# Linear attention and two MLPs on one core: ScalarE issues the stores of prepared weights, TensorE's order is written out in the direct blocks, and the last direct block's sums leave PSUM to other slots

## The chip, the cores and the metric

The kernel runs on one core of one Trainium2 chip. The metric is device time in microseconds (us), taken as the median of three runs. A core has five engines with an instruction queue each: TensorE (PE; PEld is its weight load), VectorE (DVE), ScalarE (ACT), GpSimd (POOL) and SyncE (SP), which computes nothing and issues DMAs. An engine works its queue in the order in which it was written; where an instruction waits for a semaphore, what is queued behind it waits too.

## What is computed

```python
q_s = softmax(q, over head_dim);  k_s = softmax(k, over seq)     # 8 batches, 8 heads, 576 x 64
kv  = einsum('bhsd,bhse->bhde', k_s, v)
x   = einsum('bhsd,bhde->bhse', q_s, kv)  -> 4608 tokens x 512
x   = relu(x @ w_in)**2 @ w_out                                  # 512 -> 2048 -> 512
out = (silu(x @ w_gate) * (x @ w_val)) @ w_out2                  # 512 -> 1536 -> 512
```

All arrays are float32 but the weights come in as 64-bit floats, whose bits are turned into float32 on the chip. Each float32 operand is split into a high half (`L116`, a cast on ScalarE) and a low half (`L117`, a subtraction on VectorE or GpSimd), and each product is three matmuls, high x high, high x low, low x high (`L122`, `mm3`).

## The kernel before

The 4608 tokens are nine blocks of 512. Blocks 0 to 4 go through the first MLP directly; blocks 5 to 8 in two pairs, each with seven products in place of eight (a Strassen scheme of halves); then the second MLP runs over five groups of blocks in the same scheme.

**Block 0** (to about 130 us) has an order written out by hand on all engines. **Blocks 1 to 4** (`for n in range(NF, NE * NF + LAG)`) have one step for each of the 16 slices f of the hidden layer: `h_mm` makes 12 matmuls into PSUM tile ph, `g_of` turns them into g (Relu, Square and the cast on ScalarE, the low half on VectorE), and `acc_mm` of the slice before (LAG = 1) adds 12 matmuls into four accumulators. Between them stands a tick of a clock (`first_tick`), two in each step, 128 in the four blocks. A tick runs what is due: a part of `kv_unit` and `q_unit` (attention of batches and blocks to come: loads of k, v and q, exponentials, transposes, sums; its result x goes to DRAM array x1d one tick late, through `store` and `flush`), the loads of the next block's x (`x_loads`, three ticks ahead of its first step), and a step or two of `work`.

**`work`** prepares weight operands. For the first MLP, 16 items (`first_operands`): load two tiles wsum from DRAM, four sums and differences on GpSimd, then two stages. For the second, 18 items (`operands`): load wraw, convert the bits (wbits), sums, then four stages. A stage takes the staging tile wst (one buffer in these blocks), splits a source into it and stores it to DRAM in one or two stores of 256 KB (arrays hd, ad, gvd, od). Two stages of a `first_operands` item hold two stores each; of an `operands` item, three hold two and one holds one. `Stream.fetch` loads these operands (wu) later, ahead of the products of the pairs and groups.

Order: SyncE issues in the order of the program everywhere (`manual_schedule(engines={SP})` around all). In block 0 every engine does, in the pairs TensorE does too. In blocks 1 to 4 a planner sets the order of TensorE, VectorE, ScalarE and GpSimd by its own model of their times.

Stores of operands go through `store` (L238 to L241), on SyncE at once while `hold[0]` is 0, which is so until the end of block 4. In the pairs `hold[0]` is 2: a store is put into `late` and issued two ticks later by `flush` (L243 to L246). After an `operands` item, `if late` makes two empty steps and a flush.

Slots: pool cv has one tag, wbits, with five buffers, for wbits, wsum, e of `q_unit`, the tiles of `x_loads` (four a block), x of the first pair (`x_begin`: four for c = 0, then four for c = 1) and e of `x2_store`, where each block's four accumulators leave PSUM. rp (tag r) and gp (tag g) have two buffers each and are used by `g_of`. After block 4 the accumulators' PSUM banks go to the pairs.

Of the kernel before, what the change touches and what calls it, by code (L numbers as in the profile page):

```python
# [8 lines left out]
F32 = mybir.dt.float32  # L9
F32R = mybir.dt.float32r  # L10
# [7 lines left out]
P = 128  # L18
# [4 lines left out]
def tile_linear_attention_two_mlps(  # L23
# [29 lines left out]
    nc = tc.nc  # L53
# [4 lines left out]
    T = 512  # L58
    TJ = T // P
    NB = NT // T  # L60
    NP = H // 2
    NF = FF // P
# [6 lines left out]
    def f32(ap):  # L69
        return ap.bitcast(F32)  # L70
# [166 lines left out]
    def store(to, src, ticks=0):  # L237
        if ticks:  # L238
            late.append((clock.now + ticks, to, src))
        else:  # L240
            nc.sync.dma_start(to, src)  # L241

    def flush(until=None):  # L243
        for x in list(late):
            if until is None or x[0] <= until:
                nc.sync.dma_start(x[1], x[2])  # L246
                late.remove(x)

    stages = [(stp, "wst")]
    staged = [0]  # L250
    hold = [0]

    def stage():
        pool, tag = stages[staged[0] % len(stages)]
        staged[0] += 1
        if len(stages) == 1:
            flush()
        return pool.tile([P, 2, 2, U], F32R, name="wst", tag=tag)

    made = set()  # L260
# [1 line left out]
    def operands(kind, f):  # L262

        w, by_rows = {"gate": (w_gate, False), "val": (w_val, False), "out": (w_out2, True)}[kind]
        raw = []
        for s in (f, NG + f):
            t = raws.tile([P, T], w.dtype, name="wraw", tag="wraw")
            raw_load(w, by_rows, s, t)
            raw.append(t)
        yield  # L270
        first, = bits_of(raw[:1])
        yield
        second, = bits_of(raw[1:])
        yield
        a, b = first[:, 0:U], first[:, U:2 * U]
        c, d = second[:, 0:U], second[:, U:2 * U]

        def sums(n):
            t = cv.tile([P, T], F32, name="wsum", tag="wbits")
            return t, t[:, 0:U], t[:, U:2 * U]  # L280

        def tt(to, x, y, op):
            nc.gpsimd.tensor_tensor(to, x, y, op=op)  # L283

        if by_rows:

            m, t1, t3 = sums(0)
            n, t2, t4 = sums(1)
            tt(t1, b, a, ALU.subtract)
            tt(t3, d, b, ALU.subtract)  # L290
            tt(t2, t3, a, ALU.add)
            tt(t4, c, t2, ALU.subtract)
            todo = ((first[:, 0:U], ("1",)), (second, ("2", "3")), (m, ("5", "7")), (n, ("6", "4")))
        else:

            m, s1, s3 = sums(0)
            n, s2, s4 = sums(1)
            tt(s1, c, d, ALU.add)
            tt(s3, a, c, ALU.subtract)
            tt(s2, d, s3, ALU.subtract)  # L300
            tt(s4, b, s2, ALU.subtract)
            todo = ((first, ("1", "2")), (second[:, U:2 * U], ("4",)), (m, ("5", "7")), (n, ("6", "3")))
        yield
        for source, names in todo:
            k_ = len(names)
            t = stage()
            src = source.rearrange("p (k n) -> p k n", k=k_)
            hi, lo = t[:, 0:k_, 0], t[:, 0:k_, 1]
            if by_rows:
                src = src.rearrange("p k (x e) -> p k x e", e=2)  # L310
                hi, lo = (y.rearrange("p k (e x) -> p k x e", e=2) for y in (hi, lo))
            split(hi, lo, src, nc.gpsimd if k_ == 1 else None)
            for j, name in enumerate(names):
                if by_rows:
                    to = od[PRODUCTS.index(name)][:, f]
                else:
                    to = gvd[f][:, 2 * PRODUCTS.index(name) + (kind == "val")]
                store(to, f32(t[:, j]), hold[0])
            yield
        if late:  # L320
            yield
            yield
            flush()
        made.add((kind, f))

    def all_operands():
# [6 lines left out]
    def first_to(kind, f, name):  # L333
        n = PRODUCTS.index(name)
        return hd[f // 2][:, 2 * n + f % 2] if kind == "in" else ad[n][:, f]

    def first_operands(kind, f):

        m, n = (cv.tile([P, T], F32, name="wsum", tag="wbits") for _ in range(2))
        for x, t in enumerate((m, n)):  # L340
            nc.sync.dma_start(t, w1d[kind][f][:, x])
        yield
        a, b, c, d = m[:, 0:U], m[:, U:2 * U], n[:, 0:U], n[:, U:2 * U]

        def tt(to, x, y, op):
            nc.gpsimd.tensor_tensor(to, x, y, op=op)  # L346

        if kind == "in":
            tt(a, a, c, ALU.subtract)
            tt(c, c, d, ALU.add)  # L350
            tt(d, d, a, ALU.subtract)
            tt(b, b, d, ALU.subtract)
            todo = (m, ("7", "3")), (n, ("5", "6"))
        else:
            tt(d, d, b, ALU.subtract)
            tt(b, b, a, ALU.subtract)
            tt(a, d, a, ALU.add)
            tt(c, c, a, ALU.subtract)
            todo = (m, ("6", "5")), (n, ("4", "7"))
        yield  # L360
        for source, names in todo:
            t = stage()
            split(t[:, :, 0], t[:, :, 1], source.rearrange("p (k n) -> p k n", k=2))
            for j, name in enumerate(names):
                store(first_to(kind, f, name), f32(t[:, j]))
            yield
        made.add((kind + "1", f))

# [152 lines left out]
    def q_transpose(i, hp):  # L521
        pt = ps_a.tile([P, T], F32, name="pa", tag="pa")
        src = qs.pop((i, hp)).rearrange("p j h d -> p j (h d)")
        for j in range(TJ):
            nc.tensor.transpose(pt.rearrange("r (p j) -> r j p", j=TJ)[:, j], src[:, j], ident)
        t = qtp.tile([P, 2, T], F32R, name="qT", tag=f"qT{hp % 2 if i == 1 else 0}")
        split(t[:, 0], t[:, 1], pt)
        qT[i, hp] = t

    def x_sums(px, i, hp):  # L530
        t = qT.pop((i, hp))
        for p0, n, b, _ in runs(i):
            kv = kvs[b % 2]
            c = slice(p0 * TJ, (p0 + n) * TJ)
            mm3(px[:, c], (kv[:, hp, 0], kv[:, hp, 1]), (t[:, 0, c], t[:, 1, c]), True, True)

    def x_slice(i, hp, src):
        x = xp.tile([P, 2, T], F32R, name="xT", tag="xT")
        split(x[:, 0], x[:, 1], src)
        xT[i, hp] = x  # L540
# [57 lines left out]
            clock.at(s - 1, lambda hp=hp: load_q(i, hp))  # L598
            clock.at(s + 1, lambda hp=hp: q_unit(i, hp))

    gT, acc = {}, {}

    def h_mm(i, f):
        ph = ps_h.tile([P, T], F32, name="ph", tag="ph")
        for c in range(NP):
            x = xT[i, c]
            mm3(ph, w1.pair(("in", f), c), (x[:, 0], x[:, 1]), c == 0, c == NP - 1)
        return ph
# [9 lines left out]
    def acc_mm(i, f, d):  # L618
        if f == 0:
            acc[i, d] = ps_acc.tile([P, T], F32, name="acc", tag="acc")  # L620
        g = gT[i, f]
        mm3(acc[i, d], w1.pair(("out", f), d), (g[:, 0], g[:, 1]), f == 0, f == NF - 1)

    def x2_store(i, d):
        e = cv.tile([P, T], F32, name="e", tag="wbits")
        if d % 2:
            nc.vector.tensor_copy(e, acc.pop((i, d)))
        else:
            nc.scalar.copy(e, acc.pop((i, d)))  # L629
        nc.sync.dma_start(x2d[i][:, d], e)  # L630
# [371 lines left out]
    with tc.manual_schedule(engines={mybir.EngineType.SP}):  # L1002
# [236 lines left out]
            for steps in x_steps:  # L1239
                next(steps, None)  # L1240

        for n in range(NF, NE * NF + LAG):
            i, f = divmod(n, NF)
            a = divmod(n - LAG, NF)
            if i < NE:
                if f == 0:
                    for hp in range(NP):
                        if i == 1:
                            px = ps_h.tile([P, T], F32, name="ph", tag="ph")
                            x_sums(px, i, hp)  # L1250
                            x_slice(i, hp, px)
                            if hp + 2 < NP:
                                q_transpose(i, hp + 2)
                        else:
                            x_slice(i, hp, qT.pop((i, hp)))
                        acc_mm(*a, hp)
                ph = h_mm(i, f)
                first_tick()
                g_of(i, f, ph)
            if not (f == 0 and i < NE):  # L1260
                for d in range(NP):
                    acc_mm(*a, d)
            if a[1] == NF - 1:
                for d in range(NP):
                    x2_store(a[0], d)
            if i < NE:
                first_tick()
                if clock.now > LAST - 8:
                    stream.fetch()
        for _ in x_steps[0]:  # L1270
            pass
        ph1.close()
# [3 lines left out]
        pools["ps6"] = st_first.enter_context(  # L1276
            tc.tile_pool(name="ps6", bufs=1, space=PSUM, reuse_waits="tile")
        )
        hold[0] = 2
        for p in range(len(pairs)):  # L1280
            if p:
                stages.extend(((qtp, "qT0"), (qtp, "qT1")))
# [94 lines left out]
```

## Time and profile before

| | us |
|---|---|
| median of 3 runs | 1856.49 (1851.72 to 1860.39) |
| the profiled execution, its own time | 1851.19 |
| span of that execution, first to last instruction | 1849.1 |
| TensorE busy | 1680.8 (91%) |
| VectorE busy | 1112.2 (60%) |
| ScalarE busy | 871.9 (47%) |
| GpSimd busy | 462.5 (25%) |

Busy time is an average over stages with different limits. The profile says more by stage: block 0 to 130 us, blocks 1 to 4 to 702 us, the pairs and the first gated products to about 1164 us, and the rest. Where an engine is idle, the trace names what ended its wait. SPq stands for SyncE's queue. An idle engine costs nothing unless it is the one that the end waits for.

### The profile page before, as it was taken

Reading aid. Unit: us, or ns where it says so; the run is one execution under the profiler, and the core shown is the slowest. Engines: PE = TensorE matmul, PEld = TensorE weight load, DVE = VectorE, ACT = ScalarE, POOL = GpSimd, SP = SyncE. Lnnn points to the kernel's source line nnn. Section 1 sums busy time; section 2 is a strip of 40 time slices with the busy share of each in tenths; the row PEclk is TensorE's granted clock in tenths of the full one; section 3 lists DMA queues with packets and bytes.
Section 4 is the critical chain, followed back from the end, with each engine's and each line's share of the span. In section 5 each row is a group of like instructions: output and inputs, shape, how many; then the busy total and the mean of one; then the engine's idle time right before and its main releaser. Section 6 shows DMA issues by size and latency. Waiting matters only on the chain.

```text
span 1849.1 us, 23986 instructions
## 1 busy us (share of the span) xinstructions
PE 1680.8 (91%) x8210; PEld 1364.8 (74%) x8210; DVE 1112.2 (60%) x1775; ACT 871.9 (47%) x1520; POOL 462.5 (25%) x428
## 2 busy tenths in 40 slices
PE   7999937975996988998999899999999999999999
PEld 5787725654765766786777678788888888888898
DVE  8964324435455545858676866864476368446746
ACT  7764414434444444545455554543363346334434
POOL 4752222222121232225222233301200110021010
PEclk9999958986998998999999999999999999999999
DMA  9946665455546457787788889886678677766797
GB/s 303 282 159 228 211 210 162 141 156 168 162 123 187 137 187 212 219 262 269 246 286 310 292 285 307 308 247 209 214 217 240 194 216 217 237 195 204 226 380 273
DMA packets 275017, 419.99 MB, mean 227 GB/s; under 512 B 126288, under 2 KB 167248, under 8 KB 274896
## 3 DMA queue, kind: packets, MB, share of 16 engines
q1 hardware_dynamic: 274352, 418.33, 71.0%
q8 instruction: 66, 1.08, 0.2%
q14 instruction: 55, 0.45, 0.1%
q10 hardware_dynamic: 544, 0.13, 0.0%
HBM read 317.19 MB, written 101.19 MB: 226 GB/s over the span
## 4 chain that ended last, share of the span: by engine, by line
PE 59%; DMA 10%; DVE 8%; POOL 5%; ACT 4%; issue 4%; SPq 4%; POOLq 0%; DVEq 0%; ACTq 0%
PE ps L122 51%; PE ph L122 4%; PE acc L122 3%; POOL wsum L346 2%; DMA wsum<-w1d_out 2%; DVE wst L117 1%; SPq L467 1%; ACT wst L116 1%; DMA qs<-in_q_dram 1%; SPq L241 1%; DVE uo L117 1%; POOL qs L547 1%; DMA wraw<-in_moe_w_val_dram 1%; DMA wraw<-in_moe_w_out_dram 1%; DMA wraw<-in_moe_w_gate_dram 1%
## 5 line engine op out<-in xcount | busy, mean ns | idle before, releaser
L122 PE MATMUL ps<-w,wu 128*128 128x512 f32 (+1 forms) x3192 | 680.6, 375 | 16.7 <-ACT e L629 11.6
L122 PEld LDWEIGHTS ps<-w,wu 128*128 128x128 f32 x3192 | 566.8, 189 | 126.4 <-ACT e L629 12.3
L122 PE MATMUL ps<-uo,wu 128*128 128x512 f32 (+1 forms) x1932 | 428.1, 382 | 18.1 <-DVE uo L117 18.0
L122 PEld LDWEIGHTS ps<-uo,wu 128*128 128x128 f32 x1932 | 347.9, 190 | 92.6 <-DVE uo L117 23.2
L122 PE MATMUL ph<-xT,w 128*128 128x512 f32 x960 | 255.2, 411 | 15.9 <-ACT xT L116 13.4
L117 DVE TENSOR_TENSOR uo<-u,uo 128x512 fp32r<-128x512 f32 (+1 forms) x322 | 232.7, 741 | 55.1 <-ACT uo L116 54.5
L116 ACT CAST uo<-u 128x512 fp32r<-128x512 f32 (+1 forms) x322 | 186.9, 593 | 150.4 <-PE ps L122 69.9
L122 PE MATMUL acc<-g,w 128*128 128x512 f32 x960 | 248.7, 403 | 6.6 <-ACT g L116 5.4
L122 PEld LDWEIGHTS ph<-xT,w 128*128 128x128 f32 x960 | 182.7, 195 | 61.5 <-ACT xT L116 15.2
L122 PEld LDWEIGHTS acc<-g,w 128*128 128x128 f32 x960 | 179.3, 191 | 50.3 <-ACT g L116 6.4
L953 POOL TENSOR_TENSOR u<-u 128x512 f32<-128x512 f32 (+1 forms) x30 | 36.3, 1209 | 578.5 <-DVE u L949 578.5
L948 DVE TENSOR_TENSOR u<-u,ps 128x512 f32<-128x512 f32 (+1 forms) x60 | 37.9, 631 | 184.1 <-ACT u L947 184.1
L900 ACT COPY ps<-ps 128x512 f32<-128x512 f32 x126 | 72.4, 575 | 129.4 <-PE ps L122 128.0
L117 DVE TENSOR_TENSOR wst<-wsum,wst 128x512 fp32r<-128x512 f32 x68 | 58.4, 859 | 100.4 <-ACT wst L116 91.9
L116 ACT CAST wst<-wsum 128x512 fp32r<-128x512 f32 x68 | 48.4, 712 | 101.7 <-POOL wsum L346 44.2
L117 DVE TENSOR_TENSOR g<-r,g 128x512 fp32r<-128x512 f32 x64 | 49.5, 773 | 66.1 <-ACT g L116 66.1
L283 POOL TENSOR_TENSOR wsum<-wbits 128x256 f32<-128x256 f32 x36 | 32.2, 908 | 227.4 <-DVE wbits L160 178.2
L547 POOL TENSOR_TENSOR qs<-qs,qm 128x512 f32<-128x512 f32 x28 | 31.3, 1118 | 216.2 <-DVE qm L546 179.6
L346 POOL TENSOR_TENSOR wsum<-wsum 128x256 f32<-128x256 f32 x64 | 48.1, 752 | 114.0 <-DMA wsum<-w1d_out 63.0
L612 ACT ACTIVATE r<-ph 128x512 f32<-128x512 f32 x64 | 38.2, 596 | 73.8 <-PE ph L122 73.5
L117 DVE TENSOR_TENSOR w<-x,w 128x512 fp32r<-128x512 f32 (+1 forms) x78 | 60.6, 788 | 19.4 <-ACT w L116 19.0
L116 ACT CAST w<-x 128x512 fp32r<-128x512 f32 (+1 forms) x84 | 48.2, 584 | 41.3 <-DMA x<-x2d 7.7
(188 smaller groups left out, 1796.7 us busy)
## 6 DMA issues: line engine op xcount, KB each, us to landing
wu<-gvd SPq DMA_DIRECT2D x210, 512.0 KB, 4.5
wu<-od SPq DMA_DIRECT2D x105, 512.0 KB, 4.5
wu<-hd SPq DMA_DIRECT2D x56, 512.0 KB, 5.4
wu<-ad SPq DMA_DIRECT2D x56, 512.0 KB, 5.2
gvd<-wst SPq DMA_DIRECT2D x84, 256.0 KB, 2.4
od<-wst SPq DMA_DIRECT2D x42, 256.0 KB, 5.7
w<-in_moe_w_in_dram SPq DMA_DIRECT2D x16, 512.0 KB, 6.9
w<-in_moe_w_out_dram SPq DMA_DIRECT2D x16, 512.0 KB, 6.6
```

What stands on the lines that cost most here:

```text
L116: nc.scalar.copy(hi, src)
L117: (eng or nc.vector).tensor_tensor(lo, src, f32(hi), op=ALU.subtract)
L122: nc.tensor.matmul(ps, lhsT=w[s], rhs=x[t], start=start and n == 0, stop=stop and n == 2, skip_group_check=more,)
L241: nc.sync.dma_start(to, src)
L283: nc.gpsimd.tensor_tensor(to, x, y, op=op)
L346: nc.gpsimd.tensor_tensor(to, x, y, op=op)
L467: nc.sync.dma_start(t[p0:p0 + n, :, h, :], q[b, 2 * hp + h, s:s + n * TJ, :].rearrange("(p j) d -> p j d", j=TJ),)
L547: nc.gpsimd.tensor_tensor(t, t, m.unsqueeze(3).to_broadcast([P, TJ, 2, D]), op=ALU.add)
L612: nc.scalar.activation(r, ph, AF.Relu)
L900: nc.scalar.copy(x, y)
L948: nc.vector.tensor_tensor(u, u, gate, op=ALU.mult)
L953: nc.gpsimd.tensor_tensor(s1, a21, a22, op=ALU.add)
```

## The change

1. The stores of prepared operands, in `operands` and `first_operands`, are issued by ScalarE, at the place of the stage, in all stages of the kernel. `hold` goes, and so do the flush in `stage` and the two empty steps and the flush after an `operands` item. `store` and `late` stay for the other stores (x1d, pd, x2d of the pairs).
2. The loop of blocks 1 to 4 stands in `tc.manual_schedule(engines={PE})`: TensorE runs its instructions in the order in which the program writes them. The other three compute engines stay with the planner.
3. In `x2_store` the sums of the last direct block (i = 4) are copied to the two slots of r (d = 0, 1) and to the two halves of one slot of g (d = 2, 3) instead of to slots of wbits.

```diff
     def stage():
         pool, tag = stages[staged[0] % len(stages)]
         staged[0] += 1
-        if len(stages) == 1:
-            flush()
         return pool.tile([P, 2, 2, U], F32R, name="wst", tag=tag)
...
-                store(to, f32(t[:, j]), hold[0])
-            yield
-        if late:
-            yield
-            yield
-            flush()
+                nc.scalar.dma_start(to, f32(t[:, j]))
+            yield
         made.add((kind, f))
...
             for j, name in enumerate(names):
-                store(first_to(kind, f, name), f32(t[:, j]))
+                nc.scalar.dma_start(first_to(kind, f, name), f32(t[:, j]))
             yield
...
     def x2_store(i, d):
-        e = cv.tile([P, T], F32, name="e", tag="wbits")
+        if i < NE - 1:
+            e = cv.tile([P, T], F32, name="e", tag="wbits")
+        elif d < 2:
+            e = rp.tile([P, T], F32, name="r", tag="r")
+        else:
+            if d == 2:
+                tails.append(gp.tile([P, 2, T], F32R, name="g", tag="g"))
+            e = f32(tails[0][:, d - 2])
...
-        for n in range(NF, NE * NF + LAG):
+        with tc.manual_schedule(engines={mybir.EngineType.PE}):
+            for n in range(NF, NE * NF + LAG):
...
-        hold[0] = 2
```

## Rows read from the trace of the kernel before

**Rows 1.** Busy us (count) of PE, PEld, DVE, ACT, POOL; clock; DMA; by stage.

```profile
130.50:282.70 152.20, 111.92 (x567) 87.15 (x566) 54.11 (x105) 55.89 (x100) 36.68 (x45) 0.85 0.67 215
282.70:440.00 157.30, 116.56 (x600) 89.34 (x600) 66.09 (x128) 63.94 (x115) 40.26 (x48) 0.85 0.49 149
440.00:574.40 134.40, 113.82 (x598) 88.52 (x599) 73.03 (x145) 63.06 (x118) 30.87 (x35) 0.92 0.51 158
574.40:702.00 127.60, 105.74 (x494) 81.34 (x494) 59.83 (x97) 60.43 (x110) 39.13 (x36) 0.91 0.48 159
702.00:1164.40 462.40, 437.47 (x1950) 350.49 (x1950) 335.43 (x430) 240.03 (x357) 140.84 (x99) 0.98 0.84 274
1164.40:1849.10 684.70, 680.12 (x3348) 578.59 (x3348) 414.49 (x675) 291.15 (x520) 93.86 (x78) 1.00 0.75 237
```

**Rows 2.** The same view of the four gaps at the block borders.

```profile
236.00:282.70 46.70, 10.63 (x69) 7.63 (x68) 13.15 (x29) 8.61 (x17) 10.40 (x13) 0.54 0.71 222
400.40:440.00 39.60, 8.90 (x69) 6.43 (x68) 16.18 (x34) 10.66 (x20) 8.77 (x11) 0.54 0.50 152
557.00:575.00 18.00, 5.27 (x37) 4.45 (x37) 11.26 (x22) 5.01 (x10) 5.25 (x6) 0.60 0.61 175
679.00:702.00 23.00, 5.91 (x13) 3.71 (x13) 11.33 (x11) 10.45 (x19) 19.72 (x14) 0.67 0.50 189
```

**Rows 3.** Waits of SyncE's queue, whole span: us in total, times, longest us.

```profile
SPq L241 <- DVE wst L117: 185.6, 46, 11.9
...
SPq L241 <- POOL wst L117: 41.4, 9, 7.7
...
SPq L246 <- DVE e L566: 30.5, 8, 10.2
```

**Rows 4.** Timeline of the first gap: start, us, engine, line, operation [idle before].

```profile
267.52 0.81 SPq L241 DMA_DIRECT2D ad<-wst  x2
268.42 1.29 SPq L426 DMA_DIRECT2D vt<-in_v_dram  x2
...
272.04 0.45 PE L516 MATMUL pa<-vt,kt 96*64 96x65 f32 x2 [11.61 <-DMA vt<-in_v_dram]
...
276.68 8.02 SPq L1214 DMA_DIRECT2D e<-x1d  x4
```

**Rows 5.** Timeline of TensorE at full pace, two places.

```profile
113.86 2.88 PE L122 MATMUL acc<-g,w 128*128 128x512 f32 x12
116.58 0.84 PE L122 MATMUL ph<-xT,w 128*128 128x512 f32 x3
117.35 0.92 PE L516 MATMUL pa<-wraw 96*64 96x65 f32 x24
118.20 2.32 PE L122 MATMUL ph<-xT,w 128*128 128x512 f32 x9
...
386.26 0.94 PE L122 MATMUL pa<-qT,kv 128*128 128x256 f32 x6
```

**Rows 6.** Staging tile wst, 130.5 to 702: count, ns min/median/max, first to last start.

```profile
L116 ACT CAST wst<-wsum x50: 601/619/623, 142.5 to 675.9; 128x512 fp32r<-128x512 f32 x50
L117 DVE TENSOR_TENSOR wst<-wsum,wst x50: 679/692/1382, 143.2 to 676.6; 128x512 fp32r<-128x512 f32 x50
L241 SPq DMA_DIRECT2D hd<-wst x32: 319/402/869, 144.1 to 346.7; - x32
L241 SPq DMA_DIRECT2D ad<-wst x32: 319/415/448, 216.1 to 407.6; - x32
L116 ACT CAST wst<-wbits x18: 387/504/626, 417.9 to 666.6; 128x512 fp32r<-128x512 f32 x9, 128x256 fp32r<-128x256 f32 x9
...
DMA to landing us min/median/max: 2.0/2.3/5.6
```

**Rows 7.** Timeline of ScalarE at the kernel's end: its only two DMAs.

```profile
1845.37 0.89 ACTq L996 DMA_DIRECT2D out_dram<-o  x2
```

**Rows 8.** Timeline of TensorE: the first paired product after block 4.

```profile
701.95 10.34 PE L122 MATMUL ps<-w,wu 128*128 128x512 f32 x33 [11.60 <-ACT e L629]
```

More of the change, by code (lines that the diff above doesn't have):

```diff
@@ L250, in tile_linear_attention_two_mlps @@
     staged = [0]
-    hold = [0]
     def stage():
@@ L599, in attend @@
             clock.at(s + 1, lambda hp=hp: q_unit(i, hp))
-    gT, acc = {}, {}
+    gT, acc, tails = {}, {}, []
     def h_mm(i, f):
@@ L1240, in first_tick @@
                 next(steps, None)
-        for n in range(NF, NE * NF + LAG):
[L1243 to L1269, printed above, removed]
+        with tc.manual_schedule(engines={mybir.EngineType.PE}):
+            for n in range(NF, NE * NF + LAG):
+                i, f = divmod(n, NF)
+                a = divmod(n - LAG, NF)
+                if i < NE:
+                    if f == 0:
+                        for hp in range(NP):
+                            if i == 1:
+                                px = ps_h.tile([P, T], F32, name="ph", tag="ph")
+                                x_sums(px, i, hp)
+                                x_slice(i, hp, px)
+                                if hp + 2 < NP:
+                                    q_transpose(i, hp + 2)
+                            else:
+                                x_slice(i, hp, qT.pop((i, hp)))
+                            acc_mm(*a, hp)
+                    ph = h_mm(i, f)
+                    first_tick()
+                    g_of(i, f, ph)
+                if not (f == 0 and i < NE):
+                    for d in range(NP):
+                        acc_mm(*a, d)
+                if a[1] == NF - 1:
+                    for d in range(NP):
+                        x2_store(a[0], d)
+                if i < NE:
+                    first_tick()
+                    if clock.now > LAST - 8:
+                        stream.fetch()
```

## The prediction, made before the changed kernel ran

> **What bounds the kernel now.** I read the busy time by stage first [rows 1]. From 1164.4 us to the end TensorE is busy 680.1 of 684.7 us at clock 1.00: nothing that the change touches can shorten that third. From 702 to 1164.4 it is busy 437.5 of 462.4 us, so 24.9 us are open. The four direct blocks 1 to 4 (130.5 to 702 us, four rows) take 571.5 us with TensorE busy 111.9 + 116.6 + 113.8 + 105.7 = 448.0, so 123.5 us idle, at clocks of 0.85 to 0.92. No other engine is near full there: ScalarE sums to 243.3 us, VectorE to 253.1, GpSimd to 146.9. What is short is none of the engines' time; something is late.
>
> Next, where the idle time lies [rows 2]: three gaps at the borders between blocks (46.7, 39.6 and 18.0 us long, TensorE busy 10.6, 8.9 and 5.3 in them) and one at the end of block 4 (23.0 us, busy 5.9). They hold 36.1 + 30.7 + 12.7 + 17.1 = 96.6 of the 123.5 idle us, at clocks of 0.54 to 0.67; 26.9 us are scattered.
>
> Then, who is late: SyncE's queue. It issues in program order, and its store line L241 stands 185.6 us behind VectorE's low halves (46 times) and 41.4 us behind GpSimd's [rows 3], 227 us in all; by the code that line runs in blocks 1 to 4 alone. The timeline of the first gap shows the consequence [rows 4]: the stores of ad at 267.5 come first, the load of vt is issued at 268.4 and the four loads of the next block's x from 276.7 on, over 8.0 us. TensorE meanwhile sat 11.6 us for vt, and the first product of block 2 came only with that x, at the end of the gap. It had run ahead through the rest of block 1 by the planner's order and ran dry at its border.
>
> **The floor of these blocks.** Groups of twelve matmuls of 512 columns start 2.72 us apart [rows 5] (113.86 to 116.58), 226.7 ns each; blocks 1 to 4 have 4 x 16 x 24 = 1536, so 348 us. A head of attention adds 0.85 us for its 24 sums (117.35 to 118.20 there) and up to 0.94 for its six products with qT (last row there); the clock's ticks put 20 heads into these blocks, 36 us. Together 384 us, transposes left out. The busy time was 448; of that, 30.7 us lie in the gaps [rows 2] at about half clock, where at full clock I take 15, and I take 10 off for the slow matmuls just after a gap. So 448 - 15 - 10, about **422 us**, is what TensorE needs here if it isn't starved.
>
> **Part 1: stores by ScalarE.** In blocks 1 to 4 there are 50 + 18 = 68 staging casts [rows 6]. The 50 from wsum and nine from wbits hold two stores each, nine hold one: 127 stores. SyncE loses their waits (227 us) and their issue, 0.81 us for two [rows 4], so some 51 us. Its later loads (kt, vt, qs, wsum, wraw, x of the next block) move up by this. What is late next on SyncE: the stores of x1d, still there, which wait 30.5 us for e over the run [rows 3], and loads that wait for one of five wbits slots.
>
> On ScalarE each stage adds two issues, 0.89 us [rows 7], and a wait for the low half just behind the cast. That is one VectorE subtraction, 0.69 us [rows 6], about 0.8 with hand-offs, if VectorE is free; the bounds are 0 (the planner finds other work to put between) and about 1.5 us (the longest subtraction there is 1.38 [rows 6]). I take 0.8, since VectorE is busy for about half of these blocks [rows 1]. So ScalarE's load is 243.3 + 127 x 0.445 + 68 x 0.8 = 243 + 57 + 54 = 354 us, 405 at the upper bound, 300 at the lower. Against 422 us that is 71 to 96%: covered, though not amply. Behind the waiting store stands the Relu, Square and cast of g, for which acc of the next tick waits. That chain takes some 3 x 0.62 + 0.69 = 2.5 us, by casts and subtractions of the same shape [rows 6], of the 5.44 us that the two groups of twelve give it, so one stage of 0.8 + 0.89 fits into its slack of 2.9 us and two in a row (3.4 us) do not. I charge **12 us** for the blocks, the bounds being 0 and 34 pairs x 0.5 = 17, and more in the rival below.
>
> The staging buffer is still one: a stage occupies it for 0.62 + 0.69 + 0.89 + 2.3 us until landing [rows 6, 7], 4.5 us. Two stages of an item of four steps take 9.0 us; at 1.25 steps a tick and 3.3 us a tick (422 / 128) the ticks leave 10.5. So it is nearly, not quite, the pace maker.
>
> The skill's rule on this speaks against the change. The Trainium skill, DMA: Bandwidth & Descriptors, section "Issuing engines are not separate DMA queues", says that issuing from several engines saves only the issuing sequencer's time. By it about the 51 us of issue could come back, and only where they are on the path; by the rows the time that stands to be saved is the in-order wait, which the sentence doesn't count.
>
> **Part 2: TensorE in written order.** It adds no instruction. Each attention product now stands at its tick; TensorE can't run ahead of a late one, nor be held at a border by heads that the planner drew forward. The ticks leave slack: vt is loaded four ticks (some 13 us) ahead of its sums, kt four ahead of its transpose. Alone, with SyncE as late as now, it would only spread the same waiting, hence I give it 0 by itself (bounds 97 us, the gaps, in either direction). With part 1 I keep **8 us** at each of three borders: x of the next block is loaded three ticks (9.9 us) ahead, needs four of the five wbits slots, and the four issues alone took 8.0 us in the border shown [rows 4]; the bounds are 0 and 18, the shortest border gap now. So 24 us. The 26.9 scattered us stay.
>
> **Part 3: last sums to r and g.** TensorE waited 11.6 us for the copy of the last sum (ACT e L629) before the first paired product [rows 8], since e's slots were held by the eight x tiles of the first pair. r and g are free by then, so the copy follows the last matmul. Late next: the xT operands of the second half, which now load on time. I keep **4 us** of the gap's 17.1 (bounds 0 and 17).
>
> **Part 4: pairs and first output group.** The two extra yields and two-tick holds go. By the code there are 16 x 4 + 18 x 7 = 190 stores, so 190 - 127 = 63 fall behind 702 us, 28 us of issue, and their waits for the low half stand among the uo casts. ScalarE is at 240 of 462 us there and TensorE has only 24.9 us idle [rows 1]: I charge **+4 us** (bounds -10, operands ready sooner, and +28, the whole issue on the path).
>
> **The sum.** Blocks 1 to 4: 422 + 26.9 + 24 + 4 + 12 = 489, so 571.5 - 489 = 82.5 less. The profiled execution took 1851.2 us (span 1849.1): 1851.2 - 82.5 + 4 = 1773. The median of the runs shown is 5.3 us above that execution: **1778 us**.
>
> **Rivals.**
> - *Only the issue comes back.* ScalarE takes over SyncE's waiting, and the service of the blocks is nearly as late. For it: one staging buffer, ScalarE at 96% at the upper bound. Against it: the loads no longer wait behind anything of this. SyncE's issue, 51 us, is saved: 1851.2 - 51 + 5 = 1805, up to 1846 if half of it is eaten at borders and in the pairs. This is also the time that the skill's rule above would give.
> - *No change.* The sixteen items of hd and ad took from the first store at 144.1 to the last at 407.6 us [rows 6], 16.5 us each, of which two stages hold the one buffer for 9.0. If the other 7.5, load and sums, still don't overlap the stages, because all wbits slots are held, nothing moves: about 1856. Against it: two items need four of five slots.
> - *Slower.* The place is ScalarE's in-order queue before g. A stage there costs 0.8 + 0.89 us, and if the next cast stands right behind, 2.3 us of landing as well: two stages in one pair of ticks then take some 5.7 us, 2.8 over g's slack, and TensorE, now in written order, has nothing to put in. 34 such pairs cost 95 us. It decides from where more than the 82 us gained is lost, so when nearly all pairs collide and the pairs take their upper 28: 1851.2 - 82.5 + 95 + 28 + 5, about 1897. Against it: ScalarE's order is still the planner's, which may set the casts apart.
> - *Better.* Borders and handover close fully and half of the scattered waits go: 422 + 13 = 435, so 1851.2 - 136 + 5 = 1720, or a few us less with the lower bound of part 4.
>
> **How the numbers follow.** Forecast (1745 to 1805) 0.50; only the issue (1805 to 1846) 0.20; better (below 1745) 0.11; no change 0.07; slower 0.12. The range 1720 to 1846 leaves out most of the last two and a little of the better case. About 0.5% (9 us) is what a measurement of this kernel can tell from no change: faster 0.81, same 0.07, slower 0.12.
>
> **What would show it.** Right: no wait of SyncE for VectorE's wst; the three border gaps below 15 us each and the clock near 1.0 in the blocks; ScalarE's idle time before its queue's stores under 1.5 us a stage; the first paired product within some 5 us of the last acc; the stretch from the first paired product to the end as long as now, within 15 us. Wrong: g's cast behind a store with TensorE waiting for g, hundreds of times under a us or tens of times several us; a new SyncE wait (for wbits slots or e) as long as the old; TensorE waiting for uo in the pairs by over 25 us more.

## The result and the profile after

The changed kernel takes **1802.2 us** (median of four runs, 1796.1 to 1810.0) against 1857.0 before, a ratio of 0.971 [0.967, 0.975]: 55 us faster. It is in the forecast's own range (1745 to 1805), near its slow end, and 24 us above the predicted time. The profiled execution took 1802.7 us, its span is 1800.9 us.

First the view that [rows 1] shows of before, by stage: blocks 1, 2, 3, 4, then the two pairs up to the first gated product, then the rest. Columns: length, busy us (count) of PE, PEld, DVE, ACT, POOL, granted clock, DMA share, GB/s.

```profile
131.00:258.80 127.80, 112.65 (x561) 87.03 (x559) 53.92 (x106) 53.42 (x99) 40.53 (x46) 0.93 0.80 255
258.80:381.20 122.40, 111.48 (x577) 86.44 (x576) 65.52 (x123) 61.43 (x113) 41.96 (x46) 0.96 0.62 190
381.20:511.40 130.20, 113.96 (x597) 88.87 (x596) 77.19 (x148) 65.53 (x124) 32.81 (x36) 0.93 0.56 175
511.40:623.90 112.50, 103.54 (x527) 81.28 (x525) 59.52 (x99) 59.16 (x109) 38.41 (x35) 0.98 0.52 171
623.90:1015.40 391.50, 349.84 (x1519) 276.03 (x1519) 277.32 (x349) 193.89 (x285) 115.51 (x76) 0.94 0.79 256
1015.40:1800.00 784.60, 778.25 (x3781) 657.68 (x3779) 470.49 (x755) 336.48 (x591) 119.69 (x101) 1.00 0.76 241
```

Blocks 1 to 4 take 492.9 us in place of 571.5 [rows 1], 78.6 less. TensorE is busy 441.6 of them, so 51.3 us idle where 123.5 were, at clocks of 0.93 to 0.98 where 0.85 to 0.92 were. The pairs went the other way: 391.5 us. The same stretch of before, from its first paired product at 702.0 to its first gated one at 1061.4, is 359.4 us long with TensorE busy 338.1 at clock 0.97. So 32.1 us were lost: 20.4 more idle (41.7 against 21.3) and 11.7 more busy for the same number of matmuls (1519 and 1518), at a clock of 0.94. From the first gated product to the end it is 785.5 us now and 787.7 before. The sum: -78.6 + 32.1 - 2.2 + 0.5 (block 0) = -48.2, and the spans differ by 48.2 (1800.9 and 1849.1).

The waits of SyncE's queue, over the whole span (us in total, times, longest; SPq is that queue, L675 the loads of operands ahead of their products), answer to [rows 3]:

```profile
SPq L675 <- PE ps L122: 744.5, 369, 8.4
...
SPq L246 <- DVE mx L479: 52.2, 5, 13.4
SPq L246 <- ACT e L561: 44.3, 12, 7.8
```

The 227 us behind the staging tile are gone. What is late next are the stores of x1d (L246), as the prediction said. SyncE waits nearly as long as before: by this view, in blocks 1 to 4 alone and over all lines, 312.6 us in place of 334.3, of them 157.8 for stores of x1d in place of 34.1. What fell is what these waits hold up: in before TensorE stood 29.3 us in the blocks for loads of vt, here for none. The border from block 1 to block 2 shows it, in the timeline of TensorE (start, us, line, operation, [idle before]):

```profile
251.47 0.50 PE L122 MATMUL acc<-g,w 128*128 128x512 f32 x1 [2.66 <-ACT g L116]
...
255.94 3.01 PE L122 MATMUL acc<-g,w 128*128 128x512 f32 x12
258.78 0.40 PE L122 MATMUL ph<-xT,w 128*128 128x512 f32 x1
```

The last sums of block 1 run into the first product of block 2 with nothing between; the 11.6 us behind vt [rows 4] have no counterpart; the products of blocks 3 and 4 also start at the end of the last sums (381.15 and 511.41). What is left in the blocks is scattered, like the 2.66 us behind the cast of g: 15.7 us of that kind, 7.1 behind kv and 6.9 behind kf, by their releasers.

The handover from block 4 to the pairs, all engines, answers to [rows 8]:

```profile
618.39 5.53 PE L122 MATMUL acc<-g,w 128*128 128x512 f32 x23 [0.22 <-DVE g L117]
621.92 0.59 ACT L629 COPY r<-acc 128x512 f32<-128x512 f32 x1 [2.49 <-PE acc L122]
...
623.92 3.26 PE L122 MATMUL ps<-w,wu 128*128 128x512 f32 x13
```

The 11.60 us in front of the first paired product are gone; it starts at the end of the last sum. Last, the staging tile in the blocks, with the counts, ns (min/median/max) and the landing of its stores, which answers to [rows 6]:

```profile
L315 ACTq DMA_DIRECT2D gvd<-wst x63: 325/327/1348, 367.7 to 601.5; - x63
L116 ACT CAST wst<-wsum x50: 602/620/625, 144.0 to 598.8; 128x512 fp32r<-128x512 f32 x50
...
DMA to landing us min/median/max: 2.0/3.1/7.2
```

In these blocks 127 stores stand on ScalarE (SyncE issued 125 in that stretch in before, the other two behind it), where their issue sums to 52.8 us and the queue's wait in front of them to 39.3 us (2.6 at most), added up instruction by instruction. The median landing went from 2.3 to 3.1 us.

### The profile page after: what moved, and what is told of

Read it like the earlier page. It is cut to its first block, busy times and chain, and to the rows that moved or that the text cites. A ratio compares the mean times of both kernels' runs of the same rounds, so it can differ in the third digit from the quotient of the medians.

```text
span 1800.9 us, 23969 instructions
## 1 busy us (share of the span) xinstructions
PE 1685.1 (94%) x8210; PEld 1366.9 (76%) x8210; DVE 1113.8 (62%) x1775; ACT 867.4 (48%) x1520; POOL 470.1 (26%) x428
## 4 chain that ended last, share of the span: by engine, by line
PE 57%; DMA 15%; DVE 9%; ACT 5%; POOL 4%; issue 3%; SPq 2%; ACTq 1%; DVEq 0%; POOLq 0%
PE ps L122 52%; DMA gvd<-wst 3%; DMA hd<-wst 3%; PE ph L122 2%; PE acc L122 2%; DVE wst L117 2%; DVE uo L117 2%; ACT wst L116 1%; DMA ad<-wst 1%; DMA wraw<-in_moe_w_val_dram 1%; DVE w L117 1%; DMA wraw<-in_moe_w_gate_dram 1%; DMA e<-x1d 1%; POOL wsum L280 1%; POOL wsum L339 1%
## 5 line engine op out<-in xcount | busy, mean ns | idle before, releaser
L122 PE MATMUL ps<-uo,wu 128*128 128x512 f32 (+1 forms) x1932 | 436.1, 386 | 24.0 <-DVE uo L117 21.7
L122 PE MATMUL acc<-g,w 128*128 128x512 f32 x960 | 257.9, 416 | 22.0 <-ACT g L116 15.7
L122 PE MATMUL ph<-xT,w 128*128 128x512 f32 x960 | 247.7, 405 | 5.5 <-ACT xT L116 3.4
L122 PEld LDWEIGHTS acc<-g,w 128*128 128x128 f32 x960 | 185.7, 198 | 72.4 <-ACT g L116 18.9
L540 POOL TENSOR_TENSOR qs<-qs,qm 128x512 f32<-128x512 f32 x28 | 36.0, 1285 | 229.6 <-DVE qm L539 211.1
L116 ACT CAST wst<-wsum 128x512 fp32r<-128x512 f32 x68 | 48.2, 710 | 99.0 <-DMA gvd<-wst 27.3
L339 POOL TENSOR_TENSOR wsum<-wsum 128x256 f32<-128x256 f32 x64 | 52.0, 812 | 52.0 <-DMA wsum<-w1d_out 21.3
```

The lines of the kernel that those rows point to most:

```text
L116: nc.scalar.copy(hi, src)
L122: nc.tensor.matmul(ps, lhsT=w[s], rhs=x[t], start=start and n == 0, stop=stop and n == 2, skip_group_check=more,)
L540: nc.gpsimd.tensor_tensor(t, t, m.unsqueeze(3).to_broadcast([P, TJ, 2, D]), op=ALU.add)
```

## Where the pairs lost 32 us

The two pairs are eight quarters: each pair has two halves, each half its products with w_in and then those with w_out. Two quarters lost most, 11.2 and 12.0 us. The first is the second quarter of the first pair. Names there: kf are attention's scaled sums of k and v, kv their halves, which the products with qT need; qs is q on its way through the softmax, partly on GpSimd; u and uo are the hidden layer's sums and their halves. TensorE's timeline of the changed kernel there:

```profile
672.30 0.78 PE L122 MATMUL pa<-qT,kv 128*128 128x448 f32 x3
680.24 0.85 PE L122 MATMUL pa<-qT,kv 128*128 128x64 f32 x3 [7.16 <-ACT kv L116]
```

And ScalarE's, which made kv so late:

```profile
661.63 0.33 ACTq L315 DMA_DIRECT2D gvd<-wst  x1
662.00 0.85 ACT L490 ACTIVATE kt<-kt 96x768 f32<-96x768 f32 x1 [1.99 <-POOL wst L117]
667.54 0.62 ACT L116 CAST wst<-wsum 128x512 fp32r<-128x512 f32 x1 [4.69 <-DMA gvd<-wst]
668.07 1.02 ACT L826 ACTIVATE u<-ps 128x1024 f32<-128x1024 f32 x1
668.99 0.57 ACT L116 CAST qT<-pa 128x512 fp32r<-128x512 f32 x1
...
676.74 0.63 ACT L543 ACTIVATE qs<-qs 128x512 f32<-128x512 f32 x1 [5.19 <-POOL qs L540]
...
679.89 0.29 ACT L116 CAST kv<-kf 128x128 fp32r<-128x128 f32 x1
```

Read from the top: the store waits for GpSimd's low half (the 1.99 us are put to the next compute instruction, kt). Then the next staging cast waits 4.69 us for that store to land, since the first pair has one staging tile, and u and the cast of qT stand behind it. But that wait isn't what makes kv late. Behind them ScalarE stands another 5.19 us for GpSimd's qs, and kf and kv are queued behind qs. Two kernels of the experiments below tell the two apart. In e5 ScalarE issues the stores too, but waits for no landing ahead of these instructions:

```profile
670.53 0.63 ACT L547 ACTIVATE qs<-qs 128x512 f32<-128x512 f32 x1 [4.25 <-POOL qs L544]
...
673.18 0.29 ACT L116 CAST kv<-kf 128x128 fp32r<-128x128 f32 x1
```

In e4, where SyncE issues them, kf and kv stand ahead of qs:

```profile
672.03 0.30 ACT L116 CAST kv<-kf 128x128 fp32r<-128x128 f32 x1
672.99 0.63 ACT L553 ACTIVATE qs<-qs 128x512 f32<-128x512 f32 x1 [0.67 <-POOL qs L550]
```

TensorE's wait for kv is 7.16 us in the changed kernel, 5.51 in e5 and 0.79 in e4. So the order that the planner gives the engines once the stores are in ScalarE's queue makes most of it (VectorE's rd, which kf needs, also comes 1.5 us later in e5 than in e4, counted from the start of the quarter), and the landing at most some 1.7 us. Why the planner puts qs first is not shown. In before this quarter took 48.5 us at a granted clock of 1.00, here it takes 59.7 at 0.91; the experiment e11 below comes back to it.

The second is in the third quarter of the second pair, with all engines:

```profile
915.92 1.59 DVE L117 TENSOR_TENSOR wst<-wsum,wst 128x512 fp32r<-128x512 f32 x1
...
918.51 1.08 ACT L116 CAST wst<-wsum 128x512 fp32r<-128x512 f32 x1 [2.63 <-DMA od<-wst]
918.54 0.81 ACTq L315 DMA_DIRECT2D od<-wst  x2
919.39 1.11 ACT L778 COPY ps<-ps 128x1024 f32<-128x1024 f32 x1
...
920.55 4.77 PEld L122 LDWEIGHTS ps<-w,wu 128*128 128x128 f32 x12 [4.49 <-ACT ps L778]
```

A staging cast waits 2.63 us for the landing of an older store; the copy that empties a PSUM bank (L778) is queued behind it, and TensorE, whose order is written, stands for that copy (its weight loads 4.5 us, its matmuls 4.1). Neither of these is the time of the issue itself. The second is a wait of the store's chain (low half, issue, landing, next cast) that now stands in the queue of an engine that TensorE needs within a few us; the first is in the main another order of that queue. Together they are 11 of the 41.7 us idle; the rest is in smaller waits, by their releasers 21.7 us for VectorE's uo (18.0 in before) and 4.8 for the copy L785 (0.9).

## The experiments

Times are medians in us; the ratio is to runs of the kernel before on the same chip, with its 95% interval. "Blocks" is the stretch from the first product of block 1 to the first paired product, "pairs" from there to the first gated product, from one profiled execution of each kernel. Kernels with the same code in a stretch show how far these two agree: the pairs of after, e2 and e3 take 386.8 to 391.5 us, the blocks of after, e4, e5 and e11 488.3 to 492.9.

| kernel | median | ratio | blocks | pairs |
|---|---|---|---|---|
| before | 1857.0 | 1 | 571.5 | 359.4 |
| after | 1802.2 | 0.971 [0.967, 0.975] | 492.9 | 391.5 |
| e1: after, stores as before | 1856.9 | 1.001 [1.000, 1.003] | 576.8 | 361.1 |
| e2: after, planner orders TensorE | 1795.1 | 0.968 [0.966, 0.970] | 481.5 | 386.8 |
| e3: after, old slots for the sums | 1801.5 | 0.972 [0.970, 0.974] | 492.2 | 386.8 |
| e4: ScalarE in the blocks, SyncE from the pairs on | 1771.2 | 0.956 [0.954, 0.958] | 490.9 | 358.3 |
| e5: after, with the empty steps | 1799.0 | 0.972 [0.970, 0.974] | 488.3 | 382.9 |
| e6: SyncE, one tick late in the blocks | 1784.7 | 0.964 [0.962, 0.965] | 508.5 | 357.7 |
| e7: e4, planner orders TensorE | 1760.2 | 0.951 [0.950, 0.953] | 479.8 | 357.1 |
| e9: e7, GpSimd issues in the blocks | 1803.6 | 0.974 [0.972, 0.976] | 526.6 | 358.1 |
| e10: e7, GpSimd casts in the blocks | 1783.8 | 0.964 [0.961, 0.966] | 507.4 | 357.1 |
| e11: e4, ScalarE issues the late stores | 1786.7 | 0.965 [0.962, 0.968] | 492.4 | 371.8 |

### One part undone: e1, e2, e3

**e1** keeps parts 2 and 3 and gives the stores back to SyncE, as before.

```diff
-                nc.scalar.dma_start(to, f32(t[:, j]))
+                store(to, f32(t[:, j]), hold[0])
...
```

> The changed kernel with its first part undone: stores of operands by SyncE again, two ticks late from the pairs on; TensorE's written order and the slots of r and g stay. Theory A (SyncE's wait in order is what delayed the blocks, and ScalarE's waiting stores are what cost the pairs): blocks 1 to 4 take 550 to 575 us again in place of 493, the two pairs 355 to 365 in place of 392, in all about 1835 to 1850 us. Theory B (the gain of the blocks is TensorE's order): blocks stay at 490 to 510, pairs fall to about 360, in all 1770 to 1785.

Measured 1856.9 us, no difference from before. The waits of SyncE's queue are back:

```profile
SPq L241 <- DVE wst L117: 184.6, 46, 11.1
...
SPq L241 <- POOL wst L117: 39.4, 9, 6.9
```

So the whole gain is part 1's; the written order and the slots bring nothing without it.

**e2** takes the written order of TensorE out of blocks 1 to 4.

```diff
-        with tc.manual_schedule(engines={mybir.EngineType.PE}):
-            for n in range(NF, NE * NF + LAG):
+        for n in range(NF, NE * NF + LAG):
```

> The changed kernel with its second part undone: the planner orders TensorE in blocks 1 to 4 again; stores by ScalarE and the slots of r and g stay. Theory A: blocks at 490 to 515 us, since loads are no longer behind the stores; in all 1800 to 1825. Theory B: the gaps at the borders return, blocks at 550 us or more, in all 1860 or more.

Measured 1795.1, with the blocks at 481.5: part 2 costs some 7 us, 11 in the blocks. The two intervals in the table overlap, but the pair e4 and e7 below, whose intervals don't, shows the same again (1771.2 and 1760.2, blocks 490.9 and 479.8).

**e3** gives the last sums their old slots (wbits).

```diff
-        if i < NE - 1:
-            e = cv.tile([P, T], F32, name="e", tag="wbits")
-        elif d < 2:
-            e = rp.tile([P, T], F32, name="r", tag="r")
-        ...
+        e = cv.tile([P, T], F32, name="e", tag="wbits")
```

> The changed kernel with its third part undone: the last direct block's sums go through slots of wbits again. My prediction's term: up to 12 us later at the first paired product, so 1805 to 1815 us, with a wait of TensorE for ACT e before it. Rival: the x tiles of the first pair now load in time, the slots are free anyway, and it is worth under 3 us: 1800 to 1805.

Measured 1801.5, the blocks 492.2: part 3 is worth nothing that can be measured. The wait of 11.60 us [rows 8] doesn't come back without it; the first paired product of e3 follows the last sum as in the changed kernel:

```profile
622.74 3.47 PE L122 MATMUL ps<-w,wu 128*128 128x512 f32 x14
```

So the slots of wbits are free in time once SyncE's queue isn't late.

### The pairs: e4, e5, e11

**e4** lets ScalarE issue in blocks 1 to 4 only; from the pairs on, the two-tick hold, the empty steps and SyncE stay as before.

```diff
-                nc.scalar.dma_start(to, f32(t[:, j]))
+                if hold[0]:
+                    store(to, f32(t[:, j]), hold[0])
+                else:
+                    nc.scalar.dma_start(to, f32(t[:, j]))
...
```

> The changed kernel, with ScalarE's stores in blocks 1 to 4 alone; from the pairs on SyncE issues them two ticks late, with the empty steps after an item, as the kernel before did. Theory A: blocks 490 to 495, pairs back at 360 in place of 392, in all 1765 to 1778 us. Rival C (the pairs lose because of where the operand work stands when they begin, not by ScalarE's queue): pairs stay at 385 to 395, in all 1795 to 1805.

Measured 1771.2: the pairs fall to 358.3 us and the blocks keep their gain. The pairs by the view of busy time, in the columns of the first fence:

```profile
621.90:980.30 358.40, 335.93 (x1520) 266.19 (x1520) 264.62 (x333) 188.07 (x276) 100.88 (x67) 0.99 0.83 269
```

TensorE is idle 22.5 us there (21.3 in before), and the clock is back at 0.99. So all 32 us lost in the pairs belong to part 1's edit beyond block 4.

**e5** is the changed kernel with the two empty steps after each item kept from the pairs on, with ScalarE issuing.

```diff
                 nc.scalar.dma_start(to, f32(t[:, j]))
             yield
+        if hold[0]:
+            yield
+            yield
```

> The changed kernel (ScalarE stores in all stages), with the two empty steps after each operands item put back from the pairs on. It tells ScalarE's queue from the pace of the operand work as the cause of the 32 us lost in the pairs. Theory A (ScalarE's waiting stores ahead of the copies of sums and of uo): pairs still 380 to 392 us, in all 1793 to 1803. Rival C (the work is denser without the empty steps): pairs about 360, in all 1770 to 1776.

Measured 1799.0; the pairs take 382.9, and the products of the first gated group 129.2 in place of 118.9, which gives all of it back. The faster pace of the items explains 4 to 9 us of the pairs: 8.6 against the changed kernel, 3.9 against e2 and e3, whose pairs have its code.

**e11** is e4 with ScalarE in place of SyncE as the issuer of the late stores, so that the low half is there when the store's turn comes.

```diff
-                nc.sync.dma_start(x[1], x[2])
+                x[3].dma_start(x[1], x[2])
...
-                    store(to, f32(t[:, j]), hold[0])
+                    store(to, f32(t[:, j]), hold[0], nc.scalar)
```

> The run with ScalarE's stores in the blocks and SyncE's late ones after (1771 us, written order), with ScalarE as the issuer of the late ones too: in the pairs ScalarE issues each store two ticks after its stage, when the low half is done. It parts the wait from the issue. Theory (the wait for the low half ahead of the copies of sums is the price): pairs 358 to 368 us in place of 392 with ScalarE's stores at once, in all 1769 to 1780. Rival (ScalarE's issue, 18 us, or its queue as such): pairs 375 to 390, in all 1786 to 1802.

Measured 1786.7, the pairs 371.8: between theory and rival. ScalarE's wait in front of its 35 stores there fell from 19.6 us (e5) to 6.0, and the pairs by 382.9 - 371.8 = 11 us. The two differ in the place of the stores alone (and in the flush at a stage that goes with it), so the earlier place, before the low half is done, costs about 11 us, give or take the few us by which equal code differs. More than half of it can be read in one quarter, the first of the second pair (45.4 and 39.4 us): in e5 the copy of a PSUM bank (L789) stands 3.75 us behind three stores, 2.0 of them a wait and 1.7 issue, and TensorE 4.67 us for that copy; e11 has no such wait there. Another 371.8 - 358.3 = 13.5 us stay with ScalarE as issuer, and 8.8 of them lie where the first loss was. ScalarE's timeline of e11 there:

```profile
654.63 0.81 ACTq L246 DMA_DIRECT2D gvd<-wst  x2
...
658.64 0.41 ACT L116 CAST wst<-wbits 128x256 fp32r<-128x256 f32 x1
...
661.63 0.33 ACTq L246 DMA_DIRECT2D gvd<-wst  x1
...
666.57 0.62 ACT L116 CAST wst<-wsum 128x512 fp32r<-128x512 f32 x1 [3.72 <-DMA gvd<-wst]
```

and e4's, by ScalarE and by SyncE's queue:

```profile
732.30 0.41 ACT L116 CAST wst<-wbits 128x256 fp32r<-128x256 f32 x1 [2.36 <-DMA gvd<-wst]
```

```profile
727.24 1.72 SPq L246 DMA_DIRECT2D gvd<-wst  x2
```

Both kernels write the store two ticks after its stage. On SyncE, which follows the program, it came at 727; on ScalarE, whose order is the planner's, the pair of stores stands at 654.6, as early as without the two ticks (654.62 in the changed kernel); the cast at 666.57 waits for a landing again, qs stands ahead of kf and kv again, and TensorE waits 6.19 us for kv. That quarter takes 57.3 us in e11, 59.7 in the changed kernel, 58.0 to 59.2 in e2, e3 and e5, and 48.5 in before, e1, e4, e6, e7, e9 and e10, in each of which SyncE issues the stores of the pairs. How the 13.5 us divide between issue (15.2 us on ScalarE, not all on the path), this early staging and the other order of ScalarE was not taken apart.

### The blocks: e6, e7, e9, e10

**e6** asks whether it is the issuing engine or the wait. Its edit is shown against e1. SyncE issues all stores; in the blocks it does so one tick after the stage (`hold` 1), when the low half is mostly there.

```diff
-    hold = [0]
+    hold = [1]
...
-        if late:
+        if hold[0] > 1 and late:
...
-                store(first_to(kind, f, name), f32(t[:, j]))
+                store(first_to(kind, f, name), f32(t[:, j]), hold[0])
```

> The run with SyncE's stores and TensorE's written order (1857 us), with one edit: in blocks 1 to 4 too SyncE issues a store a tick after its stage, or where the staging tile is needed again, in place of at once. Theory A (what delays the blocks is that loads stand behind a store that waits, whoever issues it): blocks fall from 577 to 500 to 535 us, in all 1780 to 1815. Rival (it takes another issuing engine, SyncE's issue time and queue being the limit): blocks 560 or more, in all 1840 to 1857.

Measured 1784.7: faster than the changed kernel as a whole, with blocks of 508.5. No issue leaves SyncE here, yet against e1 576.8 - 508.5 = 68 us are gone. The two differ by the tick, and in the blocks by the two empty steps that e1 makes after an `operands` item when a store of x1d is pending. Blocks 1 and 2, where by far the most items are of `first_operands` and have no empty steps, give 58 of the 68 (322.0 to 263.7), so the tick makes most of it. Its queue still waits:

```profile
SPq L246 <- DVE wst L117: 107.3, 36, 7.6
...
SPq L246 <- POOL wst L117: 33.2, 8, 7.5
```

140 us in place of 224. ScalarE's blocks (490.9 in e4) are 18 us better still.

**e7** is e4 without the written order, the best of what the others showed.

```diff
-        with tc.manual_schedule(engines={mybir.EngineType.PE}):
-            for n in range(NF, NE * NF + LAG):
+        for n in range(NF, NE * NF + LAG):
```

> ScalarE's stores in blocks 1 to 4 alone, SyncE's late stores from the pairs on, slots of r and g, and the planner's order of TensorE in the blocks. Theory: the written order costs what the run without it showed, 7 to 11 us in the blocks, and the two effects add: blocks about 480, pairs 360, in all 1758 to 1766. Rival: with the pairs mended the order makes no difference, 1768 to 1774.

Measured **1760.2 us**, 0.951 of before and 42 us faster than the change as it was made.

**e9** is e7 with GpSimd issuing in the blocks, to take the waiting stores off ScalarE.

```diff
-                    nc.scalar.dma_start(to, f32(t[:, j]))
+                    nc.gpsimd.dma_start(to, f32(t[:, j]))
...
```

> As the run before it in this list, with GpSimd in place of ScalarE issuing the stores of blocks 1 to 4. If what is left open in the blocks is ScalarE's queue (TensorE waits for ACT g, kv and kf, some 35 us), it goes in part: blocks 460 to 475, in all 1745 to 1758. Rival: the wait for the landing of the one staging tile is what holds ScalarE, and GpSimd's own waits delay qs and wsum: blocks 480 to 500, in all 1762 to 1785.

Measured 1803.6, the blocks 526.6, 47 us worse than e7. The waits of ScalarE in front of its staging cast (whole span):

```profile
ACT wst L116 <- DMA gvd<-wst: 88.2, 31, 8.0
...
ACT wst L116 <- DMA ad<-wst: 33.1, 11, 5.4
...
ACT wst L116 <- DMA hd<-wst: 27.1, 9, 4.5
```

In e7 the same three rows read 40.3, 16.1 and 22.1 us. The store waits in GpSimd's queue for VectorE's low half (67.6 + 43.4 + 39.4 us), it lands later by that, and ScalarE's next cast waits for the landing instead. TensorE's waits in the blocks for ScalarE's g, kf and kv rise from 24.2 us in e7 to 51.7.

**e10** is e7 with the high half cast by GpSimd in the blocks, so that this wait for the landing isn't on ScalarE.

```diff
-        nc.scalar.copy(hi, src)
+        if pool_hi:
+            nc.gpsimd.tensor_copy(hi, src)
+        else:
+            nc.scalar.copy(hi, src)
...
```

> The fastest run so far (ScalarE's stores in blocks 1 to 4, SyncE's late ones after, planner's order: 1760 us), with the high half of the staging tile made by GpSimd in the blocks, so that GpSimd and not ScalarE waits for the landing of the one tile. Theory D (what is left open in the blocks is ScalarE held by that landing, 69 us of its waits, ahead of g, kv and kf): TensorE's waits for those halve, blocks 455 to 465 us in place of 480, in all 1737 to 1747. Rival: GpSimd's waits delay the sums and qs, as where it issued the stores: blocks 485 or more, in all 1765 to 1800.

Measured 1783.8, the blocks 507.4, 28 us worse than e7. The landing is now waited for on GpSimd:

```profile
POOL wst L117 <- DMA gvd<-wst: 76.6, 19, 8.2
POOL wst L117 <- DMA hd<-wst: 47.0, 11, 6.4
...
POOL wst L117 <- DMA ad<-wst: 44.0, 13, 6.8
```

and ScalarE's stores wait 151 us for the low half (34 in e7), since the cast before it is later. Taking one link of the chain to another engine made each of the two kernels worse. A second staging tile, which would cut the link from landing to cast, wasn't tried.

## Why the prediction was right, and where it was off

**What was late.** Right. SyncE's in-order wait for the low halves was the cause: e1 brings it back with the full 55 us, e6 removes most of it with SyncE still issuing. A sum of waits is not the measure of it, though: 227 us of them went, 79 us were gained, and SyncE's waits for other things grew by 205 us. The mark "a new SyncE wait as long as the old" was a poor sign for that reason; the wait for x1d's stores came to 157.8 us in the blocks, and nothing that TensorE needed soon stood behind it.

**Blocks 1 to 4.** Forecast 489 us, measured 492.9. The terms behind it hold too, roughly: issue on ScalarE 52.8 us where 57 were put, waits for the low half 39.3 where 54 were put, 0.58 us a stage against the 1.5 given as the mark. The three borders and the handover closed fully. Idle time was put at 26.9 + 24 + 4 + 12 = 67 us and measured 51.3; TensorE's need was put at 422 (its own sum, 448 - 15 - 10, gives 423) and measured 441.6, since the clock came up to 0.93 to 0.98 only, not near 1.0 as the mark said: 93 of the 1536 matmuls of h and acc ran mostly at the lower clock (1.2 GHz) and took 18.6 us longer than at 226.7 ns each, added up instruction by instruction. The two errors nearly cancel, so the sum is better than its parts. (The upper bound of ScalarE's load, put at 405 us, is 402 by its terms.)

**Part 2.** Given 0 by itself, "with part 1" it was meant to close the borders. It isn't needed for that: e2 and e7 have blocks of 481.5 and 479.8 us without it, and it costs some 7 us (e2 against the changed kernel; 11 in e4 against e7). By releasers, TensorE's idle time in the blocks falls from 50.7 us (e4) to 41.4 (e7), above all where attention's products wait for kv (9.9 to 5.9) and qT (5.9 to 2.8).

**Part 3.** Given 13 us (the last gap's 17.1 less the 4 kept), with the 11.6 us of [rows 8] as its reason; worth nothing (e3). The wait [rows 8] was SyncE's lateness again, seen at the last place: the slots were held by x tiles whose loads were late. I counted one cause as two edits' gain.

**Part 4: the step that failed.** The pairs were charged +4 us with an upper bound of +28, the whole issue on the path; measured +32.1, above the bound. The bound counted only what ScalarE does for a store, 63 x 0.445. It left out what stands behind the store and behind the staging cast, such as the 2.63 us of landing in front of the copy L778, handed on to TensorE as 4.1; it left out that the planner would order ScalarE otherwise with the stores in its queue (kv behind qs, 7.16 us of TensorE in place of 0.79); and it left out the 11.7 us by which the same matmuls ran longer, at a clock of 0.94 in place of 0.97. The first of the three is the mechanism of my rival *slower*, which I priced for the blocks, before g, and not for the pairs, where TensorE's order is written and staging, u, kv and the PSUM copies share ScalarE; the second I had not thought of. The mark for it, TensorE waiting for uo by 25 us more, was the wrong place as well: that wait rose from 18.0 to 21.7 us only. With the measured +32.1 in place of +4, the sum gives 1773 + 28 = 1801 for the profiled execution, which took 1802.7. That term carries the miss; its price by steps is 4 to 9 us for the empty steps (e5), 11 for the stores that stand there before their low half (e11), 13.5 for ScalarE as issuer (e4), the last not taken apart.

**The rivals.** *Only the issue comes back* put 1805 us, and 1802 is nearer to it than to my 1778; it still isn't what happened. The blocks gave 78.6 us, more than the 51 us of issue, and e6 gives 68 with no issue moved. The Trainium skill, DMA: Bandwidth & Descriptors, section "Issuing engines are not separate DMA queues", says that issuing from several engines saves only the sequencer's time for it. An estimate by that sentence, with the 51 us of the rows, is the same 1805. The rows don't agree with "only", with 78.6 us gained in the blocks: what was saved is the time that loads stood behind stores that waited. *No change* is what e1 measures, with part 1 left out. *Better* (1720) isn't reached by any kernel; e7's 1760 lies 40 us above it.

**Profile and median.** The profiled execution of after lies 0.5 us above its median, that of before 5.8 below the 1857.0 it is compared with; that is 6.3 of the 6.5 us by which the medians (54.7) differ more than the spans (48.2).

## What to carry to other kernels

A store that waits for its data in an in-order queue costs what stands behind it: look at that before asking which engine has time for the issue, and try it later in the same queue first (one tick gave most of 68 us here). The sum of a queue's waits doesn't tell; what the bottleneck waits for does. When such a store is moved to a compute engine, price every stage in which it runs by what that engine's queue holds for the bottleneck, the landing wait of the next user of the buffer included, read the order that a planner gives that queue afterwards, and move the store only where there is slack. One cause can show in several gaps; count its gain once.

## What had not been expected of the hardware

- In the blocks the landing of the same stores became slower when other queues issued them: median 2.3 us by SyncE [rows 6], 2.7 by SyncE a tick late (e6), 3.1 by ScalarE, 3.6 by GpSimd (e9). The DMA engines carry more in these kernels (185 to 203 GB/s over the blocks in e6, e7 and e9, 169 in e1), so the queue alone isn't shown to be the cause. In the pairs it is the other way: median 5.7 us by SyncE (before), 5.0 by ScalarE (after).
- A store's issue occupied GpSimd for 0.54 us (median, e9), ScalarE for 0.33 to 0.42 (after) and SyncE for 0.38 to 0.42 (medians of e1 by array).
- Where the pairs had more short stalls, their matmuls were also busy longer: 1519 of them for 349.8 us at a granted clock of 0.94, with 41.7 us idle, and 1520 for 335.9 at 0.99, with 22.5 idle, in e4.
- The same operation of GpSimd (qs in the pairs, 128 x 512) took from 1.04 to 4.36 us in the changed kernel, and 1.04 to 2.63 in e4. What slowed it wasn't taken apart.
